# Attention followed by a mixture of experts on one core: the low halves of the last x block go to GpSimd and wait in the background queue, and the last w2 sum is formed and split earlier, into a freed operand

## The chip, the cores and the metric

One core of one Trainium2 chip runs the whole program. The metric is the device time of one execution in microseconds (us). TensorE (PE) multiplies, VectorE (DVE), ScalarE (ACT) and GpSimd (POOL) prepare operands and drain PSUM banks, SyncE (SP) issues most DMAs.

## What is computed

```python
# q, k, v: 4 batches x 8 heads x 576 x 64; heads 0-3 see a window of 32 keys,
# heads 4-7 every fourth key of a window of 128
scores = where(mask, q @ k.T / 8, -1e9)
x = softmax(scores) @ v                      # as rows: 2304 x 512
p = domain_probs / (domain_probs.sum(-1) + 1e-9)
for e in range(4):                           # all four experts, dense
    h = maximum(x @ w1[e], 0)                # 2304 x 1024
    out += p[:, e:e + 1] * (h @ w2[e])       # 2304 x 512
```

Everything is fp32.

## The kernel before

**Products.** Each fp32 operand is split into a high half (`...h`, rounded by ACT, L142 or L999) and a low half (`...l`, what is left, subtracted by POOL or DVE, L139 or L1000). A product is then three matmuls: high by high, high by low, low by high. The 2304 rows are three blocks of 768 (0, 1, 2), the 16 slices of 256 hidden columns are called units. Both layers use a seven-product scheme of the Strassen kind: for w1 and x there are sums (`A11`, `A12`, `A22`, `S1` to `S4` of the weights; `B11`, `B21`, `B22`, `T1` to `T4` of x), for w2 sums `P1` to `P7`. One such first-layer product is six matmuls of 128x384.

**First pass.** Attention fills the x blocks one after the other (tiles `xr`), while the expert layers already run on block 0, unit 0 to 11. From unit 2 on a unit is `mm1_a` (products A12 and A11), then `mm1_b` (S2, S1, S3, S4, A22), then its second layer, `mm2`: six tiles of 128x512 (`m`, L716), each added to `acc` by DVE (L697). The order on PE is: A12 of the next unit, three `mm2` tiles of this one, A11 of the next unit, three more tiles, then the next unit's `mm1_b`. In `mm1_b` DVE adds the S3 bank (L645) and the S4 bank (L650); the hidden halves `hh` (ACT, L598) and `hl` (DVE, L604) and the next product in the same bank follow from these. The `mm2` tiles have two PSUM buffers until `begin()` runs.

**Preparation.** The sums of x (`x_sums`, DVE, L257), the splits of x (`x_part`), of w1 (`g1h`, `g1l`: A11, A12, A22; `g2h`, `g2l`: S1 to S4) and of w2 are generators. They stand in one of two lists, `queue` and `later`, and `step()` advances the first entry of a list by one piece. `need(...)` advances both lists until the named entry is done. Between two pieces of PE work the schedule calls `step()` a few times by rules on what the expert generator yielded (`"room"`, `"full"` or nothing). Each engine executes in program order. A block's x has two halves, `i = 2m` and `2m + 1`: of block 2, half 4 and half 5. Of each the low half is made by POOL for even `i`, by DVE for odd `i`.

**Second pass.** From about 249 us `second_pass` goes over the remaining pairs of unit and block in groups. `m1` makes the same seven products with stored weights (`s_A`, `s_S`), ACT copies banks into `g` (L891 to L903), DVE adds banks to them (L893, L899, L901), `hi` (L911) and `lo` (L918, L923) split the hidden sums, `m2` (L957) runs the seven products with the halves of w2 (`w_P` in the trace). Those are made by `w2_parts`, a step at a time: ACT rounds (L999), POOL subtracts (L1000) and forms the sums in place in the raw tile `r` (L1004 to L1017). The last two of `W2_PLACES`, P7 and P4, share the tag `w2l`, P3 and P2 the tag `w2h`, with two buffers each.

**Second-round pace.** The attention turns are interleaved with `PACE` pieces of expert work per new block of heads.

Of the kernel before, what the change touches and what calls it, by code (L numbers as in the profile page):

```python
# [11 lines left out]
ALU = mybir.AluOpType  # L12
# [9 lines left out]
PACE = 7  # L22
# [26 lines left out]
def kernel(  # L49
# [212 lines left out]
    def x_part(i, n):  # L262


        m, j = divmod(i, 2)
        d = {"T1": "11", "T3": "12", "T2": "22", "T4": "21"}.get(n, n[1:])
        hi, lo = (t[:, :, j * TC:(j + 1) * TC] for t in x_op(m, "T4" if n == "X12" else n))
        split(hi, lo, quarter(i, d), nc.vector if i % 2 else nc.gpsimd)
        yield


# [354 lines left out]
    def mm1_b(k):  # L626
        u, m = k
        x, u2, s5 = st.pop(k), tmp("u2"), tmp("s5")

        def ready(n):  # L630
            if u == visits[0][0]:
                need_x(m, (n,))

        ready("T2")
        product(x, u, "S2", m, "T2", False)
        nc.scalar.activation(out=u2, in_=x, func=AF.Copy)
        yield "room"
        y = bank("x")
        ready("T1")
        product(y, u, "S1", m, "T1", True)  # L640
        nc.scalar.activation(out=s5, in_=y, func=AF.Copy)
        yield "room"
        ready("T3")
        product(x, u, "S3", m, "T3", False)
        nc.vector.tensor_tensor(out=s5, in0=x, in1=s5, op=ALU.add)  # L645
        yield
        ready("B22")
        product(y, u, "S4", m, "B22", False)
        h_hi(k, "22", s5)
        nc.vector.tensor_tensor(out=u2, in0=y, in1=u2, op=ALU.add)  # L650
        h_lo(k, "22", s5)
        h_out(k, "12", u2)
        yield "full"
        ready("T4")
        product(x, u, "A22", m, "T4", False)
        h_out(k, "21", x)
        yield "full"
# [80 lines left out]
    def experts(begin):  # L738

        for half in range(2):  # L740
            for n in ("X12", "B22") if half else ("B11", "B21"):
                for i in range(2):
                    need(x_part, i, n)
            if half == 0:
                for u in range(2):
                    need(w1_split, u)
                    yield from plain((u, 0), half)
                    need(w2_late, u)
                    yield from mm2((u, 0), u == 0, False, half, range(2))
                yield from pause("open")  # L750
        yield from plain((0, 0), 1)
        prepare(w1_split, 2)
        prepare(w1_sums, 2)
        fetch_w1(3)
        halves = plain((1, 0), 1)
        yield next(halves)
        yield from mm2((0, 0), True, False, 1, range(2))
        prepare(w2_late, 2)
        yield from halves
        for j in (1, 0):  # L760
            prepare(x_part, j, "T4", soon=True)
        need(w1_split, 2)
        need(w1_sums, 2)
        prepare(w1_late, 2, soon=True)
        opening = mm1_a(visits[0])
        yield next(opening)
        tiles = mm2((1, 0), False, False, 1, range(2))
        yield next(tiles)
        yield from opening
        yield from tiles  # L770
        prepare(w1_split, 3)
        prepare(w1_sums, 3)
        for i, (u, _) in enumerate(visits):
            end = u == LAST
            need(w1_late, u)
            keep_w1(u, True)
            parts = mm1_b((u, 0))
            yield next(parts)
            if end:
                yield next(parts)  # L780
                for n in ("T4", "T3"):
                    for j in (5, 4):
                        prepare(x_part, j, n, soon=True)
            yield from parts
            if u > LAST - len(X_PARTS):
                away_x(X_PARTS[u - LAST - 1])
            if end:
                break
            prepare(w1_late, u + 1)
            if u == 2:  # L790
                prepare(w2_late, 3)
            if u + 2 <= LAST:
                prepare(w1_split, u + 2)
                prepare(w1_sums, u + 2)
            need(w1_split, u + 1)
            opening = mm1_a((u + 1, 0))
            yield next(opening)
            need(w2_late, u)
            yield from mm2((u, 0), False, False, 1)
            begin()  # L800
            yield from opening
            if u + 1 == LAST:

                assert "m1" in gate
                need(x_sums, 5)
                for n in ("T2", "T1"):
                    for j in (4, 5):
                        prepare(x_part, j, n)
            yield from mm2((u, 0), False, False, 0)
            if u + 2 <= LAST:  # L810
                prepare(w2_late, u + 2)
        need(w2_late, LAST)
        ends = [mm2((LAST, 0), False, True, half) for half in (1, 0)]
        yield from second_pass(tile for half in ends for tile in half)
# [128 lines left out]
    def m2(g, n):  # L943

        factor, chain, begins, (i, j) = PARTS[n]
        if begins:
            sums[chain] = [
                pools["n2"].tile([128, 512], F32, tag=f"{chain}{k}", name=f"{chain}{k}")
                for k in range(2)
            ]  # L950
        banks = sums[chain]
        tiles = [banks[t // 2][:, t % 2 * 256:t % 2 * 256 + 256] for t in range(3)]
        w = w2s[n]
        for t, to in enumerate(tiles):
            ops = [(low, c, x) for low in range(2) for c in range(2) for x in range(2 - low)]
            for k, (low, c, x) in enumerate(ops):
                nc.tensor.matmul(  # L957
                    to, h_places[factor][low][:, c, t * 128:(t + 1) * 128], w[:, x, c],
                    start=begins and k == 0 and t != 1, stop=k == len(ops) - 1,
                    skip_group_check=True,  # L960
                )
        if g.m not in acc_t:
            acc_t[g.m] = pools["acc"].tile([128, TB // 128, DM], F32, name=f"acc_{g.m}")
        d = slice(j * 256, j * 256 + 256)
        for t, po in enumerate(tiles):
            at = 3 * i + t
            tt = g.m * (TB // 128) + at
            weigh_out(acc_t[g.m][:, at, d], po, tt, g.e, g.first and n in FIRST)
            if g.last and n in ("P3", "P7", "P2", "P4"):
                (nc.scalar if g.n == len(groups) - 1 and n[1] in "24" and t == 1 else nc.sync).dma_start(  # L970
                    out=out[tt * 128:(tt + 1) * 128, d], in_=acc_t[g.m][:, at, d]
                )
# [9 lines left out]
        nc.sync.dma_start(out=r, in_=w2_rows(u))  # L982
        raw_pair.append(r)

    def w2_parts():

        one, two = slice(0, DM // 2), slice(DM // 2, DM)
        b11, b12, b21, b22 = (r[:, :, d] for r in raw_pair[:2] for d in (one, two))
        del raw_pair[:2]

        def split2(n, src):
            if n not in w2s:
                tag = W2_PLACES[n]
                w2s[n] = wp.tile(
                    [128, 2, 2, DM // 2], F32R, tag=tag, name=f"w2_{n}",
                    bufs=2 if tag[0] == "w" else 1,
                )
            h, l = w2s[n][:, 0], w2s[n][:, 1]
            nc.scalar.activation(out=h, in_=src, func=AF.Copy)  # L999
            nc.gpsimd.tensor_tensor(out=l, in0=src, in1=h.bitcast(F32), op=ALU.subtract)  # L1000

        tt = nc.gpsimd.tensor_tensor
        split2("P1", b11)
        tt(out=b11, in0=b12, in1=b11, op=ALU.subtract)  # L1004
        yield
        split2("P5", b11)
        tt(out=b11, in0=b11, in1=b22, op=ALU.subtract)
        yield
        split2("P6", b11)
        yield  # L1010
        split2("P3", b22)
        tt(out=b12, in0=b22, in1=b12, op=ALU.subtract)
        yield
        split2("P7", b12)
        yield
        split2("P2", b21)
        tt(out=b21, in0=b21, in1=b11, op=ALU.add)  # L1017
        yield
        split2("P4", b21)
        yield  # L1020

    def w1_again(u, r):
# [35 lines left out]
    def second_pass(tiles):  # L1058
# [33 lines left out]
        for n in range(len(groups) + 1):  # L1092
# [20 lines left out]
            def background(b):  # L1113
# [4 lines left out]
                if n + 1 in begins:  # L1118
# [8 lines left out]
                            assert not again  # L1127
                        fetch_w2_half(runs2[run][0][b - 2], spare and spare[b - 2] or None)
                    elif b == 6:
                        w2_steps.append(w2_parts())  # L1130
                if n and again and next(again[0], 0) == 0:
                    again.pop(0)
                    next(again[0], 0) if again else None
# [91 lines left out]
    with tc.manual_schedule():  # L1225
# [319 lines left out]
        for n in range(START + 1, at(len(steps) - 1) + 2):  # L1545
# [49 lines left out]
            turns, begun = turn(new, old, n == OPEN, loaded), False  # L1595
            if n > OPEN:
                next(turns)
            left = PACE * len(new) or PACE
            while left > 0 or turns:
                left -= 1  # L1600
                full = next(ffn)
# [15 lines left out]
        for full in ffn:  # L1617
# [3 lines left out]
                step()  # L1621
            if full == "room":
                room()
            elif full != "full":
                step(later)


# [53 lines left out]
```

## Time and profile before

| | us |
|---|---|
| median of 3 runs | 801.44 (801.32 to 801.9) |
| the profiled execution, its own time | 801.16 |
| its span in the trace | 799.2 |
| PE busy in the span | 784.1 (98%) |
| DVE / POOL / ACT busy | 615.0 / 412.4 / 361.8 |

The span leaves out about 2 us that the time has around it. Busy time of PE is nearly the whole span, so what can be won is idle time of PE: it is found by its waits, stretch by stretch. The granted clock of PE is 0.9 or more of full speed in all 40 slices of the page.

### The profile page before, as it was taken

How to read it: one execution, taken by the hardware profiler on the slowest of the kernel's cores; microseconds unless marked ns; L12 is line 12 of the kernel's file. 1: busy time of each engine (PE TensorE's matmuls, PEld its weight loads, DVE VectorE, ACT ScalarE, POOL GpSimd, SP SyncE). 2: the span in 40 equal slices, each digit the busy share in tenths (PEclk: the TensorE clock that was granted, in tenths of full speed). 3: DMA queues.
4: the chain of work that ended last, by engine and by line, in shares of the span. 5: the costliest groups of instructions: out<-in, count | busy, mean ns of one | idle time of the engine just before them, and what ended most of it. 6: DMA issues, size and time to landing. Idle time of an engine off the chain costs nothing.

```text
span 799.2 us, 18123 instructions
## 1 busy us (share of the span) xinstructions
PE 784.1 (98%) x6998; PEld 745.2 (93%) x6998; DVE 615.0 (77%) x1267; ACT 361.8 (45%) x723; POOL 412.4 (52%) x388
## 2 busy tenths in 40 slices
PE   7999999999999999999999999999999999999997
PEld 5788888888888999999999999999999999999997
DVE  6787567666687767977887977887978888698787
ACT  5554554554544444444445444434334444343341
POOL 5546787887696435643915743813404560052250
PEclk9999999999999999999999999999999999999999
DMA  9768876887576666565565575574454447975612
GB/s 255 219 174 238 269 211 211 280 289 261 188 263 208 224 217 197 178 228 174 186 222 187 185 234 178 182 219 123 120 185 149 147 128 256 362 238 172 212 39 80
DMA packets 108560, 161.59 MB, mean 202 GB/s; under 512 B 8873, under 2 KB 57513, under 8 KB 108475
## 3 DMA queue, kind: packets, MB, share of 16 engines
q1 hardware_dynamic: 107771, 159.88, 62.8%
q8 instruction: 56, 0.92, 0.5%
q10 hardware_dynamic: 704, 0.56, 0.2%
q14 instruction: 29, 0.24, 0.1%
HBM read 119.25 MB, written 41.16 MB: 201 GB/s over the span
## 4 chain that ended last, share of the span: by engine, by line
PE 87%; DVE 7%; POOL 2%; ACT 2%; issue 1%; DVEq 0%; POOLq 0%; ACTq 0%
PE m1x L579 27%; PE x L957 18%; PE m1y L579 14%; PE y L957 14%; PE m L716 10%; PE po L435 2%; DVE acc L697 1%; DVE xr L257 1%; PE sc L346 1%; DVE sm L360 1%; PE pt L415 1%; POOL sm L404 1%; DVE hl L604 1%; DVE xl_B L139 0%; DVE su L391 0%
## 5 line engine op out<-in xcount | busy, mean ns | idle before, releaser
L1000 POOL TENSOR_TENSOR w_P<-r,w_P 128x512 fp32r<-128x512 f32 x70 | 95.3, 1361 | 234.1 <-ACT w_P L999 146.3
L939 DVE SCALAR_TENSOR_TENSOR g<-g 128x768 f32<-128x768 f32 x72 | 92.5, 1285 | 0.6
L697 DVE SCALAR_TENSOR_TENSOR acc<-x,pn,acc 128x256 f32<-128x256 f32 x198 | 83.1, 472 | 6.8 <-PE x L957 6.8
L697 DVE SCALAR_TENSOR_TENSOR acc<-y,pn,acc 128x256 f32<-128x256 f32 x156 | 65.5, 474 | 20.7 <-PE y L957 20.2
L579 PE MATMUL m1x<-xh_B,s_A 128*128 128x384 f32 x288 | 73.6, 337 | 0.0
L1049 POOL TENSOR_TENSOR again<-r,again 128x256 fp32r<-128x256 f32 x42 | 41.7, 993 | 60.7 <-ACT again L1048 47.1
L697 DVE SCALAR_TENSOR_TENSOR acc<-m,pn,acc 128x512 f32<-128x512 f32 x66 | 49.0, 747 | 28.0 <-PE m L716 28.0
L957 PE MATMUL x<-w_P,xh_T 128*128 128x256 f32 x432 | 69.2, 282 | 0.0
L957 PE MATMUL y<-w_P,h0h 128*128 128x256 f32 x432 | 69.1, 282 | 0.0
L999 ACT ACTIVATE w_P<-r 128x512 fp32r<-128x512 f32 x70 | 44.0, 628 | 52.5 <-POOL r L1017 16.1
L911 ACT ACTIVATE h0h<-g 128x768 fp32r<-128x768 f32 x36 | 30.3, 843 | 69.0 <-DVE g L939 69.0
L957 PEld LDWEIGHTS y<-w_P,h0h 128*128 128x128 f32 x432 | 61.0, 189 | 0.1
L957 PEld LDWEIGHTS x<-w_P,xh_T 128*128 128x128 f32 x432 | 61.1, 189 | 0.0
L716 PE MATMUL m<-w2h,hh 128*128 128x512 f32 x144 | 59.0, 409 | 1.7 <-DVE acc L697 1.1
L579 PE MATMUL m1x<-xh_T,s_S 128*128 128x384 f32 x224 | 57.0, 335 | 0.0
L716 PE MATMUL m<-w2l,hh 128*128 128x512 f32 x144 | 56.6, 393 | 0.0
L923 DVE TENSOR_TENSOR h0l<-g,h0h 128x768 fp32r<-128x768 f32 x36 | 38.2, 1061 | 22.9 <-ACT h0h L911 22.9
L579 PE MATMUL m1y<-xh_B,s_S 128*128 128x384 f32 x208 | 53.2, 337 | 0.1
L579 PEld LDWEIGHTS m1x<-xh_B,s_A 128*128 128x128 f32 x288 | 51.3, 188 | 0.0
L579 PE MATMUL m1x<-xl_B,s_A 128*128 128x384 f32 x144 | 48.4, 336 | 0.0
L716 PE MATMUL m<-w2h,hl 128*128 128x512 f32 x144 | 45.2, 393 | 0.0
L895 ACT ACTIVATE g<-m1y 128x384 f32<-128x384 f32 x36 | 17.6, 489 | 60.3 <-PE m1y L579 60.3
(215 smaller groups left out, 2250.3 us busy)
## 6 DMA issues: line engine op xcount, KB each, us to landing
s_S<-w SPq DMA_DIRECT2D x144, 256.0 KB, 3.0
s_A<-w SPq DMA_DIRECT2D x108, 256.0 KB, 3.0
r<-w SPq DMA_DIRECT2D x49, 512.0 KB, 4.2
w<-again SPq DMA_DIRECT2D x42, 256.0 KB, 3.2
v_s<-vw SPq DMA_DIRECT2D x48, 192.0 KB, 5.5
w<-g2h SPq DMA_DIRECT2D x10, 512.0 KB, 5.0
w<-g2l SPq DMA_DIRECT2D x10, 512.0 KB, 5.8
k_s<-kT SPq DMA_DIRECT2D x21, 224.0 KB, 5.3
```

What stands on the lines that cost most here:

```text
L435: nc.tensor.matmul(po[k][64 * j:64 * j + 64, o:o + QB], v_s[rows, j, 2 * i + half, :], ts_[rows, c:c + QB], start=True, stop=True,)
L579: nc.tensor.matmul(bank, w[:, k], x[:, k], start=(first and k == 0 and n == 0), stop=(last and k == 1 and n == len(parts) - 1), skip_group ...
L697: nc.vector.scalar_tensor_tensor(out=acc, in0=po, scalar=pn[:, tt, e:e + 1], in1=acc, op0=ALU.mult, op1=ALU.add,)
L716: nc.tensor.matmul(po, h, w, start=(n == 0 and x == 0), stop=(n == 3))
L895: copy(out=g.h[v, 1][:, 1], in_=to, func=AF.Copy)
L911: nc.scalar.activation(out=h_places[n][0], in_=source(g, n), func=AF.Relu if n in RAW else AF.Copy)
L923: nc.vector.tensor_tensor(out=l, in0=source(g, n), in1=h.bitcast(F32), op=ALU.subtract)
L939: nc.vector.scalar_tensor_tensor(out=g.h[n], in0=g.h[one], scalar=0.0, in1=g.h[two], op0=ALU.max, op1=op)
L957: nc.tensor.matmul(to, h_places[factor][low][:, c, t * 128:(t + 1) * 128], w[:, x, c], start=begins and k == 0 and t != 1, stop=k == len(o ...
L999: nc.scalar.activation(out=h, in_=src, func=AF.Copy)
L1000: nc.gpsimd.tensor_tensor(out=l, in0=src, in1=h.bitcast(F32), op=ALU.subtract)
L1049: tt(out=t[:, 1], in0=src, in1=t[:, 0].bitcast(F32), op=ALU.subtract)
```

## The change

It has four parts. (1) In `x_part` all low halves of block 2 go to POOL, half 5 too. (2) The four T sums' splits of block 2 (T1 to T4) go into `later` without a place in front; the `need(x_sums, 5)` ahead of them is gone; after attention is over `later` is advanced by other rules: a piece that yields `"sum"` (between S3 and S4) advances nothing, a `"full"` piece only when more than three entries stand in `later`, other pieces once, and twice with more than four. (3) The first attention turn after `OPEN` gets 8 instead of 7 pieces of expert work per head block, 16 for its two. (4) In `w2_parts` the sum for P4 is formed in `b12` instead of `b21`, right after P7's split. In the last run it is also split right there, as `"end"`, into the place of block 2's B22 operand (`xh_B22_2`, `xl_B22_2`), which is no longer used then.

```diff
@@ x_part
-        split(hi, lo, quarter(i, d), nc.vector if i % 2 else nc.gpsimd)
+        split(hi, lo, quarter(i, d), nc.vector if i % 2 and i < 4 else nc.gpsimd)
@@ mm1_b, between S3 and S4
-        yield
+        yield "sum"
@@ experts, last unit
-                for n in ("T4", "T3"):
-                    for j in (5, 4):
-                        prepare(x_part, j, n, soon=True)
+                for n in ("T3", "T4"):
+                    for j in (4, 5):
+                        prepare(x_part, j, n, of=later)
...
-                need(x_sums, 5)
                 for n in ("T2", "T1"):
                     for j in (4, 5):
-                        prepare(x_part, j, n)
+                        prepare(x_part, j, n, of=later)
@@ m2
-        w = w2s[n]
+        w = w2s["end" if n == "P4" and g.n == len(groups) - 1 else n]
@@ w2_parts
         def split2(n, src):
+            if n == "end":
+                w2s[n] = tuple(t[:, :, :DM // 2] for t in x_op(NBL - 1, "B22"))
...
         split2("P7", b12)
+        tt(out=b12, in0=b21, in1=b11, op=ALU.add)
+        if end:
+            split2("end", b12)
         yield
         split2("P2", b21)
-        tt(out=b21, in0=b21, in1=b11, op=ALU.add)
         yield
-        split2("P4", b21)
+        if not end:
+            split2("P4", b12)
         yield
@@ turns of attention
-            left = PACE * len(new) or PACE
+            left = (PACE + (n == OPEN + 1)) * max(1, len(new))
@@ after attention
-            elif full != "full":
-                step(later)
+            elif full != "sum":
+                if not full:
+                    step(later)
+                if len(later) > 3 + (not full):
+                    step(later)
```

Three places show what this does to the order on the engines. The first is DVE in unit 11, the last of the first pass: L645 and L650 drain S3 and S4, L139 with `xl_` are low halves of block 2 (`xl_B11_0` and `xl_B21_0` are tiles used again, for T3 and T4 of block 2). Before:

```order
L139 TENSOR_TENSOR xl_B11_0_420<-xr_2883,xh_B11_0_419 128x2x192
L645 TENSOR_TENSOR s5_3977<-m1y_3925,s5_3977 128x384
L650 TENSOR_TENSOR u2_3976<-m1x_3987,u2_3976 128x384
L604 SCALAR_TENSOR_TENSOR hl_4015<-s5_3977,hh_4012 128x384
L604 SCALAR_TENSOR_TENSOR hl_4019<-u2_3976,hh_4017 128x384
L139 TENSOR_TENSOR xl_T2_0_1189<-xr_2883,xh_T2_0_1188 128x2x192
L604 SCALAR_TENSOR_TENSOR hl_4031<-m1y_3925,hh_4029 128x384
L139 TENSOR_TENSOR xl_T1_0_1204<-xr_2883,xh_T1_0_1203 128x2x192
L139 TENSOR_TENSOR xl_B21_0_494<-xr_2883,xh_B21_0_493 128x2x192
L893 TENSOR_TENSOR g_4051<-m1x_4060,g_4051 128x384
```

and now:

```order
L697 SCALAR_TENSOR_TENSOR acc_0_600<-m2_3954,pn_74,acc_0_600 128x512
L697 SCALAR_TENSOR_TENSOR acc_0_600<-m2_3966,pn_74,acc_0_600 128x512
L645 TENSOR_TENSOR s5_3981<-m1y_3926,s5_3981 128x384
L650 TENSOR_TENSOR u2_3980<-m1x_3990,u2_3980 128x384
L604 SCALAR_TENSOR_TENSOR hl_4015<-s5_3981,hh_4012 128x384
L604 SCALAR_TENSOR_TENSOR hl_4019<-u2_3980,hh_4017 128x384
L604 SCALAR_TENSOR_TENSOR hl_4031<-m1y_3926,hh_4029 128x384
L892 TENSOR_TENSOR g_4051<-m1x_4060,g_4051 128x384
```

No low half stands ahead of L645 any more, and the four that stood here are on POOL.

The second is POOL during unit 10, behind the w2 low half of the unit: `g2l` are the low halves of S2, S1, S3, S4 of unit 10, `g1l` those of A11, A12, A22 of unit 11, `xl_` those of block 2. Before:

```order
L139 TENSOR_TENSOR g2l_3719<-r1_3341,g2h_3718 128x256 x2
L139 TENSOR_TENSOR xl_B11_2_3762<-xr_1814,xh_B11_2_3761 128x2x192
L139 TENSOR_TENSOR g2l_3719<-r1_3341,g2h_3718 128x256 x2
L139 TENSOR_TENSOR xl_B21_2_3788<-xr_1814,xh_B21_2_3787 128x2x192
L139 TENSOR_TENSOR g1l_3802<-r1_3598,g1h_3801 128x256 x2
L139 TENSOR_TENSOR xl_B22_2_3821<-xr_2883,xh_B22_2_3820 128x2x192
L139 TENSOR_TENSOR g1l_3802<-r1_3598,g1h_3801 128x256
L178 TENSOR_TENSOR r1_3598<-r1_3598 128x2x128
```

and now:

```order
L139 TENSOR_TENSOR g2l_3719<-r1_3338,g2h_3718 128x256 x2
L139 TENSOR_TENSOR xl_B11_2_3762<-xr_1828,xh_B11_2_3761 128x2x192
L139 TENSOR_TENSOR xl_B11_2_3762<-xr_2892,xh_B11_2_3761 128x2x192
L139 TENSOR_TENSOR g2l_3719<-r1_3338,g2h_3718 128x256
L139 TENSOR_TENSOR xl_B21_2_3778<-xr_1828,xh_B21_2_3777 128x2x192
L139 TENSOR_TENSOR xl_B21_2_3778<-xr_2892,xh_B21_2_3777 128x2x192
L139 TENSOR_TENSOR g2l_3719<-r1_3338,g2h_3718 128x256
L139 TENSOR_TENSOR xl_B22_2_3794<-xr_2892,xh_B22_2_3793 128x2x192
L139 TENSOR_TENSOR g1l_3808<-r1_3597,g1h_3807 128x256
L139 TENSOR_TENSOR xl_B22_2_3794<-xr_2892,xh_B22_2_3793 128x2x192
L139 TENSOR_TENSOR g1l_3808<-r1_3597,g1h_3807 128x256 x2
```

The `g2l` and `g1l` rows now have six low halves of x ahead of or between them instead of two or three, and in unit 11, further down the same engine, the four low halves of T2 and T1 stand in a row as POOL's last work ahead of the second pass.

The third is ACT in the last run of the second pass: L897 (now L896) copies the PSUM bank of S2, which the product S3 then overwrites. Before:

```order
L999 ACTIVATE w2_P7_4194<-r_9232 128x512
L897 ACTIVATE g_9629<-m1x_9598 128x384
L911 ACTIVATE xh_T3_0_1215<-g_9646 128x768
L999 ACTIVATE w2_P2_4311<-r_9281 128x512
L911 ACTIVATE h0h_4253<-g_9465 128x768
L903 ACTIVATE g_9552<-m1x_9598 128x384
L999 ACTIVATE w2_P4_4361<-r_9281 128x512
```

and now:

```order
L1001 ACTIVATE w2_P7_4194<-r_9232 128x512
L1001 ACTIVATE xh_B22_2_3793<-r_9232 128x2x256
L896 ACTIVATE g_9629<-m1x_9598 128x384
L910 ACTIVATE xh_T3_0_1215<-g_9649 128x768
L1001 ACTIVATE w2_P2_4312<-r_9281 128x512
L910 ACTIVATE h0h_4254<-g_9465 128x768
L902 ACTIVATE g_9552<-m1x_9598 128x384
```

The split for P4 has moved from behind L903 to the row ahead of the copy, and it waits for POOL.

## Rows read from the trace of the kernel before

**Rows 1.** The page, busy time of the engines.

```profile
PE 784.1 (98%) x6998; PEld 745.2 (93%) x6998; DVE 615.0 (77%) x1267; ACT 361.8 (45%) x723; POOL 412.4 (52%) x388
```

**Rows 2.** Waits of PE by cause, 205 to 260 us.

```profile
PE m1y L579 <- DVE s L645: 0.9, 1, 0.9
PE m1x L579 <- DVE u L650: 0.6, 1, 0.6
PE m L716 <- ACT hh L598: 0.4, 1, 0.4
```

**Rows 3.** Waits of PE by cause, 770 to 800 us.

```profile
PE x L957 <- DVE acc L697: 0.4, 1, 0.4
PE y L957 <- DVE h0l L923: 0.3, 1, 0.3
PE x L957 <- DVE h1l L923: 0.2, 1, 0.2
```

**Rows 4.** Timeline of PE around the three stalls (first column: start).

```profile
220.09 0.39 PE L716 MATMUL m<-w2h,hh 128*128 128x512 f32 x1
...
222.52 0.39 PE L716 MATMUL m<-w2h,hh 128*128 128x512 f32 x1
...
232.06 0.34 PE L579 MATMUL m1x<-xh_B,g1l 128*128 128x384 f32 x1
...
247.26 0.34 PE L579 MATMUL m1x<-xl_B,g2h 128*128 128x384 f32 x1
248.48 0.45 PE L579 MATMUL m1y<-xh_T,g1h 128*128 128x384 f32 x1 [0.89 <-DVE s L645]
...
254.20 0.51 PE L579 MATMUL m1x<-xh_T,s_S 128*128 128x384 f32 x2
```

**Rows 5.** Timeline of DVE, 210 to 256 us.

```profile
214.10 1.56 DVE L139 TENSOR_TENSOR xl_T<-xr,xh_T 128x384 fp32r<-128x384 f32 x2
...
218.52 0.56 DVE L139 TENSOR_TENSOR xl_T<-xr,xh_T 128x384 fp32r<-128x384 f32 x1 [0.39 <-ACT xh_T L142]
219.00 0.75 DVE L697 SCALAR_TENSOR_TENSOR acc<-m,pn,acc 128x512 f32<-128x512 f32 x1
...
246.75 1.21 DVE L139 TENSOR_TENSOR xl_B<-xr,xh_B 128x384 fp32r<-128x384 f32 x1
...
253.42 0.56 DVE L893 TENSOR_TENSOR g<-m1x,g 128x384 f32<-128x384 f32 x1 [0.64 <-ACT g L891]
```

**Rows 6.** Timeline of POOL in unit 10.

```profile
224.22 0.81 POOL L139 TENSOR_TENSOR g2l<-r,g2h 128x256 fp32r<-128x256 f32 x1 [1.57 <-ACT g2h L142]
224.99 1.02 POOL L139 TENSOR_TENSOR xl_B<-xr,xh_B 128x384 fp32r<-128x384 f32 x1
225.96 1.76 POOL L139 TENSOR_TENSOR g2l<-r,g2h 128x256 fp32r<-128x256 f32 x2
227.68 1.41 POOL L139 TENSOR_TENSOR xl_B<-xr,xh_B 128x384 fp32r<-128x384 f32 x1
229.03 1.45 POOL L139 TENSOR_TENSOR g1l<-r,g1h 128x256 fp32r<-128x256 f32 x2
230.43 1.04 POOL L139 TENSOR_TENSOR xl_B<-xr,xh_B 128x384 fp32r<-128x384 f32 x1
```

**Rows 7.** Timeline of ACT around the start of the second pass.

```profile
249.36 0.51 ACT L142 ACTIVATE xh_T<-xr 128x384 fp32r<-128x384 f32 x1
...
252.89 0.49 ACT L891 ACTIVATE g<-m1x 128x384 f32<-128x384 f32 x1 [1.26 <-DVE xl_B L139]
```

**Rows 8.** Timeline of all engines, 769 to 788 us.

```profile
770.68 1.29 POOL L1000 TENSOR_TENSOR w_P<-r,w_P 128x512 fp32r<-128x512 f32 x1 [0.97 <-PE m1x L579]
...
773.65 0.51 PE L579 MATMUL m1x<-xh_T,s_S 128*128 128x384 f32 x2
...
774.88 1.89 POOL L1017 TENSOR_TENSOR r<-r 128x512 f32<-128x512 f32 x1
...
779.56 2.04 DVE L939 SCALAR_TENSOR_TENSOR g<-g 128x768 f32<-128x768 f32 x1
```

More of the change, by code (lines that the diff above doesn't have):

```diff
@@ L957, in m2 @@
                 nc.tensor.matmul(
-                    to, h_places[factor][low][:, c, t * 128:(t + 1) * 128], w[:, x, c],
+                    to, h_places[factor][low][:, c, t * 128:(t + 1) * 128], w[x][:, c],
                     start=begins and k == 0 and t != 1, stop=k == len(ops) - 1,
@@ L983, in fetch_w2_half, with w2_parts @@
         raw_pair.append(r)
-    def w2_parts():
+    def w2_parts(end=False):
         one, two = slice(0, DM // 2), slice(DM // 2, DM)
@@ L991, in split2 @@
         def split2(n, src):
+            if n == "end":
+                w2s[n] = tuple(t[:, :, :DM // 2] for t in x_op(NBL - 1, "B22"))
             if n not in w2s:
                 tag = W2_PLACES[n]
-                w2s[n] = wp.tile(
+                t = wp.tile(
                     [128, 2, 2, DM // 2], F32R, tag=tag, name=f"w2_{n}",
@@ L997, in split2 @@
                 )
-            h, l = w2s[n][:, 0], w2s[n][:, 1]
+                w2s[n] = t[:, 0], t[:, 1]
+            h, l = w2s[n]
             nc.scalar.activation(out=h, in_=src, func=AF.Copy)
@@ L1129, in background @@
                     elif b == 6:
-                        w2_steps.append(w2_parts())
+                        w2_steps.append(w2_parts(run == len(runs2) - 1))
                 if n and again and next(again[0], 0) == 0:
```

## Prediction

> **What bounds the kernel now.** I read the page first, for which engine fills the span, then the waits of PE by cause in the stretches that the change touches, then the timelines of the engines named there. PE is busy for 784.1 of 799.2 us [rows 1]. So nothing that makes another engine quicker counts unless PE waits for it, and the whole idle time of PE, under 16 us, is the most that could be won. In the stretch where block 2's x is prepared, 205 to 260 us, PE has three waits, together 1.9 us, and all three end on DVE or on an `hh` that follows from DVE [rows 2]. In the last 30 us it has three more, 0.9 us together [rows 3]. The stretch between has no wait that the change could take away, so the forecast is a balance of these two places.
>
> A wait costs more than its entry. At the last of the three, the matmul of 247.26 is followed by one at 248.48 [rows 4]: 1.22 us from start to start, where two matmuls of this shape last 0.51 together and one 0.34 [rows 4], so that they follow each other in 0.17. That is 1.05 us late, and the next matmul too starts late (the row lasts 0.45 against 0.34), so I put the loss at 0.89 + 0.27 = 1.16. With the same 0.27 the three stalls cost (0.6 + 0.4 + 0.9) + 3 x 0.27 = 2.7; taken from late starts one by one I get 0.82, 0.98 and 1.16, together 2.96, which I use (2.7 stays as the low end). Call them A (unit 9, 216 us), B (unit 10, 234 us) and C (unit 11, 248 us).
>
> **What the first part takes away.** Ahead of A stand two low halves on DVE, 1.56 us [rows 5], between the drain of S3 (L645) and that of S4 (L650); ahead of C one of 1.21 us [rows 5] stands before L645. B is a low half and an L257 between the same two. The changed order has none of these there. C goes, 1.16. B goes, 0.98. A goes as a wait of the product, but DVE still has the same seven operations (three `hl`, three low halves, one `acc`) before the third `mm2` tile may have a buffer. That `acc` row is 219.00 plus 0.75, so it ends at 219.75 [rows 5], and the third tile starts at 220.09 [rows 4]. It can come forward by about 0.3 at most, with a new wait on `acc` in place of the old one: of A's 0.82, about 0.5 comes back (0.3 to 0.8).
>
> **What it adds in unit 10.** POOL starts on the second `g2l` of unit 10 at 224.22 [rows 6], which is 1.70 after A11 ends at 222.52 (the first `mm2` tile starts there [rows 4]); what it waits for, ACT behind a DVE add of A12 and A11, is the same afterwards. From there to the second `g1l` (A12 of unit 11) the old order has five weight halves and two low halves of x; the new order has five and six. Undisturbed they follow each other in 0.70 (1.40 us for the two `g1l`, 229.03 to 230.43) and 0.97 (224.99 to 225.96) [rows 6]. The old sum is 5 x 0.70 + 2 x 0.97 = 5.4; measured it is 6.26 (224.22 to 230.48), 15% more, because some rows met DVE work: 0.86 for a `g2l`, 1.35 for a low half, 227.68 to 229.03 [rows 6]. The new sum is 5 x 0.70 + 6 x 0.97 = 9.3 undisturbed and 10.7 with 15%, so `g1l` of A12 is ready 1.70 + 9.3 = 11.0 to 12.4 us after A11's end. PE needs it at 232.06, 9.54 after [rows 4]. In the old order it was ready at 7.96, with room; now it is 1.5 to 2.9 late. `g2l` of S4 is the third of the five and has four low halves ahead, 1.70 + 3 x 0.70 + 4 x 0.97 = 7.7 against a need at 9.54 - 2 x 1.05 = 7.4, so a part of the wait shows up there already, 0.2 to 0.9; it is the same lateness and not added. The low halves that left DVE no longer disturb POOL, so I take a little under the middle: 2.0.
>
> **What it adds at the start of the second pass.** In unit 11 the low halves of T2 and T1 (half 4 and half 5 of each) are POOL's alone and in a row. They cannot begin before ACT has rounded T2, and ACT does that behind `hh` of L650, 1.87 after S4 ends: the bank is drained 0.26 after, 0.55 for the add, 0.50 for `hh` up to the next row, 0.51 for the rounding (the row of 249.36 [rows 7]) and 0.05 to hand over. Four low halves of 0.97 end at 1.87 + 3.9 = 5.8. The first copy of the second pass (L891) waits for the last of them, because its tile lies where block 2's x lay. Before, the copy of 252.89 waited for DVE's last low half [rows 7], DVE added at 253.42 [rows 5], and the product S2 that needs the add started at 254.20 without a wait [rows 4]. Now copy (0.49), add (0.56) and three hand-overs take it to 6.95, or 7.25 if POOL is stretched by 0.3; S2 could start 5.61 after S4's end (254.20 less 248.48, less the 0.11 of the slow start). New wait 1.35 to 1.65; I take 1.5.
>
> **A rule beside the trace.** Two low halves took DVE 1.56 us where one alone takes 0.56 (218.52): about 0.5 more than two alone, and the L139 of 246.75 took 1.21 for one [rows 5]. The Trainium skill, SBUF — State Buffer, section "Who interferes with whom", says that a DVE instruction with two SBUF inputs contends with a GpSimd instruction that reads SBUF, and that the shared pair is an exclusive lock, so one side blocks for the other's whole instruction. This trace agrees in kind: a DVE low half beside POOL takes up to twice its time (1.21 against 0.56), and POOL's of 227.68 lasts 1.41 against 1.02. By it a low half moved to POOL holds the pair nearly twice as long as it did on DVE, which speaks against the move; the sum above has this as its 15%, and it is the slow rival below.
>
> **The tail.** In the last run ACT's split for P4 now stands ahead of the copy of the S2 bank, and waits for POOL to sum. POOL's low half of P7 is 770.68 plus 1.29, ends at 771.97; the sum (1.29 like a 128x512 row undisturbed, 1.89 like the row of 774.88) ends at 773.3, ACT's split takes 0.62, the copy 0.49 (the shape of the row of 252.89 [rows 7]) and S3, which starts at 773.65, starts at about 774.45 [rows 8]: 0.8 lost, 1.4 with the long sum. What comes back: POOL's P4 half no longer runs beside DVE's 2.04 us row at 779.56 [rows 8], and the sum of 774.88 no longer stretches the DVE work ahead of the first wait. The three waits cost 0.9 + 3 x 0.27 = 1.7 [rows 3]; about 0.9 of that goes, the wait on `h0l` at the end stays. Net -0.1, between -0.5 and +0.6. In the other runs the earlier sum moves idle time of POOL and ACT only, where PE has no wait: nothing, as long as POOL's idle time in the second pass covers the 1.3 us of a sum; uncovered it would be 1.3 per run.
>
> **The pace and the order of `later`.** One piece more per head block moves attention work back by two pieces of expert work. In the rows of order before 205 us no low half or L257 comes to stand between L645 and L650 that did not before. I price it at nothing, since PE has work of both kinds there and the sum of its work is unchanged; a stall like A, 0.8 either way, is the bound.
>
> **The sum.** Gone: 2.96. New: 0.5 + 2.0 + 1.5 = 4.0. Tail -0.1. Net +0.9 on the profiled execution's 801.16: 802.1, and with the median 0.28 above that execution, 802.3.
>
> **The rivals.** A difference of 0.2%, 1.6 us, is about what a measurement of this kernel can tell from none. *Forecast*: the stalls change places, 800.2 to 803.0, chance 0.5. *POOL keeps up*: if `g1l` of A12 is ready within 9.54 us of A11's end and the last T1 half within 4.4 us of S4's end, neither new wait exists, and 2.96 - 0.5 + 0.1 = 2.6 us are won: 798.9. It needs POOL to begin its chain 1.5 us earlier or ACT to deliver T2 earlier than the rows say. For it speaks that all old waits lie on DVE and that POOL is busy for 52% of the span only [rows 1]; against it the count of rows on POOL. With the pace also taking away a stall elsewhere, 798. Chance 0.22. *POOL and DVE block each other*: every L257 or `hl` that meets POOL's chain holds it up by its own 0.56. Three such in unit 10 and two in unit 11 give waits of 1.5 + 1.65 = 3.1 and 1.35 + 1.1 = 2.5, the tail's sum 0.6: 0.5 + 3.1 + 2.5 + 0.6 - 2.96 = +3.7, 805.2; it decides (beyond 803.0) from two such meetings more than the forecast has. The chain measured 15% over speaks for it, that DVE has lost the low halves speaks against. Chance 0.28. That the change does nothing at all in the order is excluded by the rows of order.
>
> **Range.** From 799.2, most of the way to POOL keeping up, to 804.4, most of the way to the blocked one. The forecast's own range is 800.2 to 803.0. Faster 0.22, same 0.5, slower 0.28.
>
> **What would show it.** Right: PE's waits of L650 and L645 at 216 and 248 are gone; PE waits for POOL (`g2l`, `g1l`, L139) near 230 to 233, for DVE's L892 near 253 and ACT's L896 near 774; ACT's first copy waits for POOL's `xl`. POOL's row at 779 is missing and DVE's L939 there takes about 1 us. Wrong: no PE wait for POOL in unit 10, or a start of its chain well ahead of 1.70; new waits before 205 us; a tail that loses over 1 us.

## The result and the profile after

The changed kernel takes 808.3 us (median of 6 runs, 807.14 to 809.42), the kernel before 801.92 in the runs beside it: a ratio of 1.0078, 95% interval 1.0065 to 1.0091. It is slower by 6.4 us; 802.3 was forecast, and the range ended at 804.4. The profiled execution took 808.45, its span is 806.6.

The waits of PE in the changed kernel, 205 to 270 us and then 770 to 810 us (us in total, times, longest):

```profile
PE m L716 <- DVE acc L697: 2.9, 1, 2.9
PE m1x L579 <- DVE g L892: 1.4, 1, 1.4
PE m1x L579 <- POOL g1l L139: 1.3, 1, 1.3
PE m1x L579 <- POOL g2l L139: 0.6, 1, 0.6
...
PE m1x L579 <- ACT g L896: 0.6, 1, 0.6
```

All three waits of [rows 2] and all three of [rows 3] are gone. Four of the five new ones are those that the prediction worked out, near the sizes it gave: `g2l` and `g1l` together 1.9 (2.0 was taken), L892 1.4 (1.5), L896 0.6 (0.8). The first was foreseen at the right place, the third `mm2` tile of unit 9, but at 0.5 and not 2.9.

PE around that wait, called the hole from here on (timeline, first column the start):

```profile
225.05 0.50 PE L716 MATMUL m<-w2h,hh 128*128 128x512 f32 x1 [2.86 <-DVE acc L697]
...
226.84 0.53 PE L579 MATMUL m1y<-xh_B,g1h 128*128 128x384 f32 x1
227.16 0.53 PE L579 MATMUL m1y<-xh_B,g1l 128*128 128x384 f32 x1
...
229.61 0.39 PE L716 MATMUL m<-w2h,hh 128*128 128x512 f32 x1
```

Behind it PE is slow: two matmuls of 128x384 stand 0.32 apart, where they follow each other in 0.17 elsewhere, and one takes 0.53. The windows of this kernel say why (us of the stretch, then busy time of PE, PEld, DVE, ACT and POOL, the granted clock, DMA share, GB/s):

```profile
222.00:225.00 3.00, 0.19 (x1) 0.00 (x0) 3.00 (x4) 0.25 (x1) 2.92 (x3) 1.00 0.23 82
225.00:226.00 1.00, 0.95 (x4) 0.82 (x5) 1.00 (x2) 0.00 (x0) 0.00 (x0) 1.00 0.46 164
226.00:229.00 3.00, 3.00 (x11) 2.77 (x10) 0.87 (x2) 0.00 (x0) 0.00 (x0) 0.53 0.90 326
229.00:232.00 3.00, 3.00 (x13) 2.42 (x13) 1.87 (x3) 2.41 (x7) 1.50 (x2) 0.90 0.84 317
```

The granted clock falls to about half, the lower of its two levels (1.2 GHz), after PE has stood still, and is back at 229 to 232 us. PE is nearly always busy in the kernel before, so no stretch near here showed that. Whether the hole is the cause is taken up at the run that fills it.

DVE and POOL ahead of the hole:

```profile
217.38 0.56 DVE L650 TENSOR_TENSOR u<-m1x,u 128x384 f32<-128x384 f32 x1 [0.42 <-PE m1x L579]
217.85 1.09 DVE L604 SCALAR_TENSOR_TENSOR hl<-s,hh 128x384 fp32r<-128x384 f32 x1
218.87 1.09 DVE L604 SCALAR_TENSOR_TENSOR hl<-u,hh 128x384 fp32r<-128x384 f32 x1
219.88 1.09 DVE L139 TENSOR_TENSOR xl_T<-xr,xh_T 128x384 fp32r<-128x384 f32 x1
220.90 0.54 DVE L604 SCALAR_TENSOR_TENSOR hl<-m1y,hh 128x384 fp32r<-128x384 f32 x1
221.37 2.96 DVE L139 TENSOR_TENSOR xl_T<-xr,xh_T 128x384 fp32r<-128x384 f32 x2
224.26 0.74 DVE L697 SCALAR_TENSOR_TENSOR acc<-m,pn,acc 128x512 f32<-128x512 f32 x1
...
218.60 0.93 POOL L182 TENSOR_TENSOR r<-r 128x256 f32<-128x256 f32 x1
219.62 0.94 POOL L184 TENSOR_TENSOR r<-r 128x256 f32<-128x256 f32 x1
221.09 2.83 POOL L139 TENSOR_TENSOR w2l<-r,w2h 128x512 fp32r<-128x512 f32 x2 [0.53 <-ACT w2h L142]
```

The seven DVE operations ahead of the tile are those that the prediction counted. From the first `hl` to the end of `acc` they take 7.15 us (217.85 to 225.00). At the undisturbed times, 0.54 to 0.56 for six and 0.74 for `acc`, they would take about 4. Two low halves, 1.1 alone, took 2.96 beside POOL's two w2 halves; before, only one of the three low halves stood between L650 and this `acc`, and it ended as POOL's w2 half began (219.08); two had run ahead of L650 [rows 5].

The two low halves and the two w2 halves one by one (timeline in narrow windows):

```profile
221.37 1.43 DVE L139 TENSOR_TENSOR xl_T<-xr,xh_T 128x384 fp32r<-128x384 f32 x1
222.72 1.61 DVE L139 TENSOR_TENSOR xl_T<-xr,xh_T 128x384 fp32r<-128x384 f32 x1
...
221.09 1.29 POOL L139 TENSOR_TENSOR w2l<-r,w2h 128x512 fp32r<-128x512 f32 x1 [0.53 <-ACT w2h L142]
222.34 1.58 POOL L139 TENSOR_TENSOR w2l<-r,w2h 128x512 fp32r<-128x512 f32 x1
```

POOL's rows end at 222.38 and 223.92, and DVE's end 0.41 to 0.42 behind them, at 222.80 and 224.33. The same holds for the rows of 217.85, 218.87 and 219.88, each with the POOL row that it met. So an `hl` or a low half that starts beside a running POOL row is held until that row is over, however long it is. The `hl` that reads a PSUM bank (`m1y`) is not: in the kernel before it took 0.55 at 217.59, inside a POOL row that ran from 217.33 to 218.27.

**Where the 7.4 us of the two spans come from**, by how much later the same instruction starts than before. The `acc` of 91.46 starts 1.6 later; up to there the order of all engines is nearly the same, and the kernels of the experiments, with that same order, were 0.3 to 2.5 late there, so this is put down to variation of the start-up, which no run shows by itself. The `acc` of 210.41 is 2.8 late: 1.2 lost between 94 and 145 us. The copy of S2 in unit 10 (L636, 227.96 before) is 6.6 late: 3.8 lost at the hole of unit 9. The DVE row of 266.19 is 8.5 late: 1.9 in unit 10, unit 11 and the start of the second pass. The row that stood at 783.57 is 7.9 late: 0.6 won in the tail. The last 0.5 is in the output's DMAs.

### The profile page after: what moved, and what is told of

It reads as the page before. It is cut to its first block, busy times and chain, and to the rows that moved or that the text cites. A ratio compares the mean times of both kernels' runs of the same rounds, so it can differ in the third digit from the quotient of the medians.

```text
span 806.6 us, 18110 instructions
## 1 busy us (share of the span) xinstructions
PE 785.8 (97%) x6998; PEld 745.9 (92%) x6998; DVE 612.4 (76%) x1260; ACT 362.9 (45%) x723; POOL 417.8 (52%) x395
## 4 chain that ended last, share of the span: by engine, by line
PE 66%; DVE 1%; POOL 0%; ACT 0%; issue 0%; DVEq 0%
PE m1x L579 23%; PE x L956 19%; PE y L956 14%; PE m1y L579 9%; PE m L716 1%; DVE acc L697 0%; POOL r L1017 0%; POOL w_P L1002 0%; DVE xl_T L922 0%; POOL xl_T L139 0%; ACT xh_T L910 0%; ACT xh_B L1001 0%; DVE g L892 0%; DVE g L938 0%; ACT g L890 0%
## 5 line engine op out<-in xcount | busy, mean ns | idle before, releaser
L1002 POOL TENSOR_TENSOR w_P<-r,w_P 128x512 fp32r<-128x512 f32 x69 | 98.0, 1422 | 223.5 <-ACT w_P L1001 124.1
L938 DVE SCALAR_TENSOR_TENSOR g<-g 128x768 f32<-128x768 f32 x72 | 87.6, 1217 | 0.6
L1054 POOL TENSOR_TENSOR again<-r,again 128x256 fp32r<-128x256 f32 x42 | 39.6, 943 | 66.3 <-ACT again L1053 65.1
L956 PE MATMUL x<-w_P,xh_T 128*128 128x256 f32 x420 | 67.2, 282 | 0.0
L956 PEld LDWEIGHTS x<-w_P,xh_T 128*128 128x128 f32 x420 | 59.4, 189 | 0.0
```

The source lines that it names most:

```text
L938: nc.vector.scalar_tensor_tensor(out=g.h[n], in0=g.h[one], scalar=0.0, in1=g.h[two], op0=ALU.max, op1=op)
L956: nc.tensor.matmul(to, h_places[factor][low][:, c, t * 128:(t + 1) * 128], w[x][:, c], start=begins and k == 0 and t != 1, stop=k == len(o ...
L1054: tt(out=t[:, 1], in0=src, in1=t[:, 0].bitcast(F32), op=ALU.subtract)
```

## The experiments

Each kernel was profiled and timed against the kernel before; the times of before in these runs are 802.6. The changed kernel's 808.3 was measured beside 801.92; what comes back is counted from 808.3 below, and would be 0.7 more if each kernel were counted from the before beside it. The four parts are called pace (part 3 of the change), rules (the list order, the missing demand and the drain rules, part 2), low halves (part 1) and sum (part 4). "Undone" is relative to the changed kernel.

**Pace undone.**

```diff
-            left = (PACE + (n == OPEN + 1)) * max(1, len(new))
+            left = PACE * len(new) or PACE
```

> The change with its pace undone (7 pieces per head block in the second round again). In the trace of the change PE falls behind by 1.2 us between 90 and 145 us, where the first order of PE differs, and by 3.8 us in unit 9, where three hl and three low halves stand ahead of the first acc on DVE. With the old pace one of the three low halves stands ahead of L650 again. Theory (the new pace moves work against POOL's w2 halves): the 1.2 us and about 1.5 of the 3.8 come back, 805.6 us against 808.3. Rival (the drain rules alone make the wait of unit 9, the 1.2 us are chance): 808.

Measured: 803.62, ratio 1.0012 (1.0003 to 1.0022): 4.7 us come back (5.0 by the lateness in the two traces, from 94 us to the end), more than the theory gave. The loss between 94 and 145 us is gone (the lateness stays at 2.5 from 94 to 165 us), and so is the whole hole of unit 9. This is also the kernel for which the prediction's sum was made, since it priced the pace at nothing: +0.9 was worked out, +1.0 measured, with `g2l` 0.9, `g1l` 1.3, L892 1.5 and L896 0.6 as PE's waits. That the two numbers meet is in part luck. The sum put a late restart of 0.27 on each old wait and none on the new ones, which bring it too: in the changed kernel the matmul behind the 1.28 of `g1l` starts 1.62 after the one ahead of it instead of 0.17, and the next one 0.28 after that, 1.56 in all. Three of these make 0.8, which the tail (0.6 won, not 0.1) and A (0.5 won, not 0.3) make up for in the main. The DVE and POOL rows of its unit 9:

```profile
219.27 1.09 DVE L139 TENSOR_TENSOR xl_T<-xr,xh_T 128x384 fp32r<-128x384 f32 x1
220.28 0.55 DVE L604 SCALAR_TENSOR_TENSOR hl<-m1y,hh 128x384 fp32r<-128x384 f32 x1
220.75 0.62 DVE L139 TENSOR_TENSOR xl_T<-xr,xh_T 128x384 fp32r<-128x384 f32 x1
221.30 0.74 DVE L697 SCALAR_TENSOR_TENSOR acc<-m,pn,acc 128x512 f32<-128x512 f32 x1
...
220.94 3.16 POOL L139 TENSOR_TENSOR w2l<-r,w2h 128x512 fp32r<-128x512 f32 x2
```

Its last low half ahead of `acc` starts 0.2 us before POOL's w2 half, takes 0.62, and POOL's pair takes 3.16 instead of 2.83. In the changed kernel the two start 0.3 us behind it and take 2.96. This kernel also has one low half fewer between L650 and `acc`, because one ran ahead of L650 (at 216.76). Whether the number of low halves or the half microsecond of phase between the two engines keeps the hole away was not tried by itself.

**Low halves on DVE again.**

```diff
-        split(hi, lo, quarter(i, d), nc.vector if i % 2 and i < 4 else nc.gpsimd)
+        split(hi, lo, quarter(i, d), nc.vector if i % 2 else nc.gpsimd)
```

> The change with the low halves of half 5 on DVE again. Theory (POOL's queue makes the waits on g2l and g1l in unit 10, 0.6 and 1.3 us, and the wait on L892 at the start of the second pass, 1.4): all three go, with 0.27 of restart each, unless DVE's low halves bring a wait of about 0.5 back: 804.5 to 805 us. The wait of unit 9 (2.9) stays, since these are low halves of block 1. Rival (DVE and POOL block each other wherever the low halves run): 807 to 808, with waits on DVE in place of those on POOL.

Measured: 806.75 (1.0037 to 1.0067), 1.6 us back, between theory and rival. PE's waits, 205 to 270 us:

```profile
PE m L716 <- DVE acc L697: 2.8, 1, 2.8
PE m1y L579 <- DVE s L645: 2.6, 2, 1.9
```

The waits on POOL and on L892 go, as the theory says, so POOL's queue made them. But 2.6 us of waits on DVE take their place, not 0.5. The hole of unit 9 stays, and the granted clock falls behind it (0.50 from 226 to 229 us).

**Rules undone.** The edits of part 2 taken back:

```diff
-        yield "sum"
+        yield
...
+                need(x_sums, 5)
...
-            elif full != "sum":
-                if not full:
-                    step(later)
-                if len(later) > 3 + (not full):
-                    step(later)
+            elif full != "full":
+                step(later)
```

> The change with the list order, the demand for all sums and the drain rules of before. In unit 9 DVE then has three hl and one low half ahead of the first acc instead of three. Theory (those low halves, slowed beside POOL's w2 halves, make the wait of 2.9 us and through it the slow clock behind): both go, 3.8 us, the wait on L645 in unit 11 of before may come back (1.2): 804.5 to 805.7 us. Rival (the wait comes from POOL's or DVE's total work, whatever stands first): 808.

Measured: 805.9 (1.0023 to 1.0053), 2.4 us back. The hole is gone, as the theory says: at 210 us this kernel is 2.6 late, at 224 us 2.4. The time falls less, since the wait at the start of the second pass grew to 2.4 (on L893), and the granted clock fell behind it (0.50 from 260 to 262 us); L645 has none.

**Sum undone.** The lines of `w2_parts` and `m2` of before.

> The change with the last w2 sum formed and split as before. In the trace of the change the last 30 us gain 1.1 us against before although a wait of 0.6 on L896 is new. Theory (POOL's P4 half no longer beside DVE's rows): undone it costs 1.1 us, 809.4. Rival (the gain is chance, or nothing but the wait on L896 counts): 807.5 to 808.3.

Measured: 808.84 (1.0066 to 1.0102), 0.5 more (0.1 less against the before beside it), which the timing cannot tell from no change. The trace can: its DVE rows are 7.60 late at 769 us and still 7.60 at 783 us, with the three waits of [rows 3] back, while the changed kernel goes from 8.43 to 7.89. The earlier sum is worth 0.5 to 0.6 us, half of what was expected here.

**The hole filled.** The second tile is multiplied three times, into its own bank:

```diff
-            for n, (c, low) in enumerate([(c, low) for low in range(2) for c in cs]):
+            for n, (c, low) in enumerate(
+                [(c, low) for low in range(2) for c in cs] * (3 if (u, half, i) == (9, 1, 1) else 1)
+            ):
+                n %= 4
```

> The change, with the second mm2 tile of unit 9's first three multiplied three times over into its own bank (the output is the same): 2.8 us of matmuls in the hole of 2.9 us in which PE waits for the first acc. In the change the granted clock is 1.00 up to the hole and 0.50 from 226 to 229 us behind it. Theory (the idle hole lets the clock fall, and the slow stretch behind costs about 1.8 us more): the clock stays at 1.00 and 1.8 us come back, 806.5 against 808.3, while DVE ends its acc as late as before. Rival (the clock falls for another reason, or the slow stretch is hidden behind a wait anyway): 808.

Measured: 807.18 (1.0037 to 1.0085), 1.1 less, which the timing alone cannot tell from no change. The windows of this kernel:

```profile
222.00:225.00 3.00, 3.00 (x14) 2.16 (x12) 3.00 (x3) 0.33 (x2) 3.00 (x3) 1.00 0.24 97
225.00:226.00 1.00, 0.85 (x5) 0.70 (x5) 1.00 (x3) 0.00 (x0) 0.05 (x1) 1.00 0.55 90
226.00:229.00 3.00, 3.00 (x16) 2.66 (x15) 1.54 (x3) 0.49 (x2) 0.00 (x0) 1.00 1.03 390
```

DVE ends its `acc` as late as before, the third tile starts at 225.16 (225.05), and the clock stays at 1.00. From there to the third matmul of the next `mm2` tile (228.19, and 229.61 in the change) it takes 3.03 us against 4.56. So the lower clock cost 1.5 us of the 3.8. That filling the hole is what kept the clock up is not shown: the kernel with the sum undone has the same hole, unfilled, and its clock stays at 1.00 as well.

```profile
225.31 0.50 PE L716 MATMUL m<-w2h,hh 128*128 128x512 f32 x1 [2.86 <-DVE acc L697]
...
226.00:229.00 3.00, 3.00 (x16) 2.63 (x15) 1.69 (x3) 0.35 (x1) 0.00 (x0) 1.00 0.98 358
```

Of the three kernels that left a hole of 2.9 in unit 9, the changed one and the one with half 5's low halves on DVE lost their clock behind it, and this one did not, each in one profiled execution. What decides between them is open.

**POOL's w2 halves in quarters**, only those that POOL makes during the hole (they are unit 10's):

```diff
+            if u == 10:
+                nc.scalar.activation(out=wh[:, c], in_=r[:, c], func=AF.Copy)
+                for d in range(4):
+                    s = slice(d * 128, d * 128 + 128)
+                    held.append((wh[:, c, s], wl[:, c, s], r[:, c, s], nc.gpsimd))
...
```

> The change, with the two w2 low halves that POOL makes during unit 9's wait cut into four pieces of 128x128 each. Theory (a DVE instruction with two SBUF inputs waits for the whole POOL instruction that is in progress): the two low halves on DVE that take 2.96 us together wait for pieces of about 0.4 and take about 2.0, so that the wait of 2.9 on acc falls to about 2 and the time to about 807.3. Rival (the two share the port evenly): the same 2.96 us and 808.3, or more for POOL's extra starts.

Measured: 805.91 (1.0026 to 1.0058), 2.4 less, more than the theory gave. Its DVE and POOL rows:

```profile
221.52 1.33 DVE L139 TENSOR_TENSOR xl_T<-xr,xh_T 128x384 fp32r<-128x384 f32 x2
222.78 0.74 DVE L705 SCALAR_TENSOR_TENSOR acc<-m,pn,acc 128x512 f32<-128x512 f32 x1
...
221.24 4.33 POOL L139 TENSOR_TENSOR w2l<-r,w2h 128x128 fp32r<-128x128 f32 x8 [0.52 <-ACT w2h L210]
```

With the same data and the same order, DVE's two low halves take 1.33 instead of 2.96, while POOL takes 4.33 instead of 2.83. The wait is 1.2 instead of 2.9, and the granted clock stays at 1.00 behind it. It is the length of POOL's single instruction that DVE pays. The Trainium skill, SBUF — State Buffer, section "Who interferes with whom", says that issue order decides which of the two blocks, and that it blocks for the whole instruction; the traces agree, here, in the ends 0.41 behind POOL's rows in the change, and in the 0.62 of the kernel without the pace.

**The pace alone**, in the kernel before (the line of the first experiment, the other way round).

> The kernel before with the new pace alone (8 instead of 7 pieces per head block in the second round). Its order on DVE in unit 9 has three hl and one low half ahead of the first acc. Theory (the pace costs 1.2 us between 90 and 145 us by itself, and the 2.9 us wait of unit 9 only together with the drain rules): 1.2 slower there, unit 9's old wait of 0.6 gone: 803.0 against 802.6. Rival (the pace alone brings unit 9's wait): 806.

Measured: 801.73, ratio 0.9988 (0.9977 to 1.0): no slower than before, and better than either expected. Its lateness rises from 0.3 at 103 us to 1.8 at 145 us, so the pace by itself loses 1.5 there, with a wait of 0.7 of `sc` on the copy of `pts`. It falls to 0.1 by 258 us, because units 9 and 11 no longer wait (only the 0.4 of B is left of [rows 2]). So the pace brings the hole only together with the rules, and neither brings it alone.

**Rules and sum alone** (pace undone and low halves on DVE).

> The change without its pace and with half 5's low halves on DVE: the drain rules, the list order and the earlier w2 sum alone. Theory (POOL's queue makes the waits on g2l, g1l and on the first sum of the second pass, 3.7 us with the pace undone): those go, DVE's low halves bring up to 2 back as they did with the pace: 801.5 to 802.5, at or under the 802.6 of before. Rival (POOL and DVE block each other either way): 803.6.

Measured: 801.3, ratio 0.9985 (0.9972 to 0.9998). From 205 to 270 us PE waits twice for L645, 1.9 together; nothing is left of the waits on POOL.

**Only T1 and T2 of half 5 on GpSimd**, otherwise as the last.

```diff
-        split(hi, lo, quarter(i, d), nc.vector if i % 2 else nc.gpsimd)
+        split(hi, lo, quarter(i, d), nc.vector if i % 2 and (i < 4 or n not in ("T1", "T2")) else nc.gpsimd)
```

> The kernel with drain rules, list order and earlier w2 sum of the change, the old pace, and of half 5 only the T1 and T2 low halves on GpSimd. With all of half 5 on DVE (and the old pace) PE waited for L645 1.4 us in unit 10 and 0.55 in unit 11, the second behind T2's low half. Theory (in unit 11 POOL has room for two more low halves, since its last T3 half starts only behind ACT): the 0.55 and its restart go, no wait on the first copy of the second pass returns: 800.5 us against 801.3 for that kernel and 802.6 before. Rival (the two more on POOL come late or block DVE): 801.5 or more, with a wait on POOL or on L892.

Measured: 801.15, ratio 0.998 (0.997 to 0.999). The wait of 0.55 is gone and none came on POOL; one wait of 1.3 on L645 in unit 10 is left. The 0.15 to the last kernel is less than the timing can tell.

**Pace and sum alone.**

> The kernel before with the new pace and the earlier last w2 sum, and nothing else of the change. The pace alone gave 801.7 against 802.6; the earlier sum gave 0.6 in the last 30 us of the change. Theory (the two add up, since one lies before 260 us and the other behind 770): 801.1. Rival (the tail's gain needs the shift that other parts brought): 801.7.

Measured: 800.65, ratio 0.9979 (0.9969 to 0.9989). The two add up at least, and this is the fastest median of the study, 0.2% under the kernel before. From 205 us to the end PE has two waits: 0.4 on `hh` in unit 10, and 0.6 on L897, the one that the earlier sum brings.

## Why the prediction was wrong

**The step that failed** is the last of "What the first part takes away", on A: that the third tile would come forward by about 0.3, with a wait of 0.5 on `acc`. It counted the right seven operations and kept the end of `acc` from the row of before, 219.75 [rows 5]. But two of them had been moved behind L650, to where POOL makes its w2 halves, and the row of before held their times beside other POOL work. The prediction had the blocking, in its rule beside the trace, but reckoned with it for POOL's chain in unit 10 and not for DVE at this place. The wait was 2.9 in place of 0.5. With the slow clock behind it, less the 0.82 of the old stall, 3.8 us were lost. In the kernel without the pace the same step comes out about right: A gains 0.5, and no wait on `acc` is recorded.

**The second** is "The pace and the order of `later`", priced at nothing with 0.8 either way as the bound. Measured from the pace alone, it loses 1.5 between 103 and 145 us and saves about as much behind 205 us; in the change it costs 4.7, because with it no low half runs ahead of L650 any more and the last two meet POOL's w2 halves. The prediction's own sign, a new wait before 205 us, is there: 0.4 on the copy of `pts`. The blocked rival had the mechanism, but it placed it in units 10 and 11; it ended on the right side, at 805.2, and its price was still too small.

**What held.** POOL's chain in unit 10: it starts 1.74 after A11's end (1.70 was taken), and from there to the second `g1l` it takes 10.4 us (230.50 to 240.87), inside the 9.3 to 10.7 worked out; the two waits sum to 1.9 against 2.0. The chain of the second pass: POOL's four low halves in a row take 4.24 (3.9 undisturbed) and the wait on L892 is 1.4 against 1.5. The tail: 0.6 of wait on L896 against 0.8, and a net gain of 0.5 to 0.6 against 0.1, at the end of the range that was given.

**A correction of names.** A table in the code (`PLACE`) puts T2 and T1 of block 2 into the tiles `xl_B11_0` and `xl_B21_0`, and T3 and T4 into `xl_T2_0` and `xl_T1_0`. The text ahead of the prediction, and the prediction, have it the other way round: the four low halves in a row ahead of the second pass are those of T3 and T4. The times do not hang on it, since the rows were counted by tile.

**What stays open.** How much of the 1.5 us between 103 and 145 us belongs to which attention step was not tried; only one wait of 0.4 to 0.7 is recorded there. The order of DVE and POOL that makes the wait on L893 2.4 in the kernel with the rules undone was not followed up. Why the clock held behind the hole in one kernel and fell in two is not known.

## What to carry to other kernels

A duration read from a trace holds for the neighbours that the instruction had there. When an edit moves it along its engine, ask what the engine that can block it does at the new place, and how long a single instruction of that engine is: here 1.1 us became 2.96, and cutting the neighbour's instruction in four gave back most of it. A hole on PE can cost twice, once as idle time and once as a lower clock behind it: 1.5 us on top of 2.9 in this change. Parts of a change that cost nothing one by one can still meet: the pace alone, and the rules with the earlier sum, were each no slower than before, and the pace and the rules together made the hole.

## What the runs showed of the hardware

After PE had stood still for 2.9 us the granted clock was about 0.5 from 226 to 229 us, 1.5 us of loss. It fell behind the same hole in the kernel with half 5's low halves on DVE, and behind the wait of 2.4 with the rules undone; it stayed at 1.00 behind the same hole with the sum undone, in the kernel that filled the hole, and behind a wait of 1.2. An `hl` or low half with both inputs in SBUF that started while a POOL row ran, more than 0.1 us before its end, ended itself 0.41 to 0.42 us behind that end: all 19 from 209 to 262 us, 10 in the kernel before and 9 in the changed one. POOL's 128x512 subtraction made a DVE subtraction of 128x384 take about 1.5 us on average where it takes 0.55 alone, and four of 128x128 in its place 0.67.
